# A recurrent attention kernel: its loads, its row stores and its feed-forward slots in a new order

## The chip, the cores and the metric

The kernel runs on one core of one Trainium2 chip. The metric is the device time of one execution in microseconds (us), lower is better. Engines are named as the profile names them: PE is TensorE (PEld its weight loads), DVE VectorE, ACT ScalarE, POOL GpSimd, SP SyncE, which here only issues DMA transfers.

## The reference

Two layers with residuals over x of 2048 tokens by 640. The first is attention in segments of 32 tokens with a memory of 8 rows that is handed from segment to segment, so the 64 segments are computed one after the other. The second is a feed-forward layer with a squared ReLU.

```python
# A: 32 heads of 128, 64 segments, M = 8, everything bfloat16
mem = mem0
for s in range(64):
    h = concatenate([mem, layernorm(x)[32 * s:32 * s + 32]])       # 40 x 640
    q, k, v = h @ Wq, h @ Wk, h @ Wv                                # 32 heads
    p = softmax(where(mask, q @ k.T * 128 ** -0.5, -1e9))
    o = (p @ v) @ Wo                                                # 40 x 640
    mem = o[:8]
    out_s = o[8:]
h = x + concatenate(out)
# B: 640 -> 1728 -> 640
h2 = h + relu(layernorm(h) @ w1 + b1) ** 2 @ w2 + b2
```

## The kernel before, in words

One step per segment, `step(s, ...)`, 64 steps; four steps (sp 0 to 3) make one block b of 128 tokens, 16 blocks. The memory rows and the first 24 tokens of a segment (the head rows) are 32 rows and go through the step's own chain: the Q, K and V products (`half`, `pass_units`), transposes of Q and K (`turn`), scores, exponent, sums, the product with V, and the product with Wo (`wo_units`, `wo_out`, tile `pw`, result tile `o`). Its first 8 rows are the memory of the next segment: `mem_to_hT` transposes them and puts them into hT, on which the next step's Q product waits. This chain cannot be overlapped with itself. The last 8 tokens of the four segments of a block (the tail rows) influence no memory, so they are computed for a whole block at once and ahead (`tail_units`, `tail_turn`) or behind (`wo_tail_units`, tile `psw`, result tile also tagged `o`).

Such work, and the feed-forward of an earlier block, is laid into the step's pauses. `slots` is a dictionary of lists of functions, run at named places of the step: "q" behind the Q product, "k" behind the K product, "v" and "d" behind the V product and the normalised weights, "w0" ahead of the Wo result, "w" at the end. `pre` and `mid` stand around the product with V, `post` around `mem_to_hT`. The feed-forward of one block is: load the rows of x (tile `ffh`) and of the attention's output (tile `ffa`), add them and take statistics (`ff_stats`), a reciprocal root (`ln_root`: 14 small operations on GpSimd), normalise (`ff_apply`), transpose (`ff_turn`), and eight pieces `ff_slot(b, p, tag)`, p = 0 to 7, each of two 128-wide chunks of the hidden layer: products with W1 (tile `psf`), ReLU on ScalarE, square on GpSimd (tile `f1`), products with W2 of the piece before (tile `acc`). A queue `ffq` holds these; `run_ff` takes one at two places of each step ("pv3" ahead of the Q and K transposes, "pv0" behind the weights). Each piece asks for the next W1 chunks (`ff_load1`, tile `w1c`, from w1d, a copy of W1 by chunks in DRAM) and its own W2 chunks (`ff_load2`, tile `w2c`).

Attention output goes through DRAM: each step stores its head rows (4 transfers), each block its tail rows (16 transfers), all to `a_rows`, and one transfer loads the 128 rows of a block.

Weights are loaded once. Each of Wq, Wk and Wv has 640 rows, held as five chunks of 128 partitions; the first four are four transfers, the fifth is gathered from four places: ScalarE's queue copies it to a scratch tensor `w4s` in DRAM, and SyncE's queue loads it from there. Wo comes in four transfers, two by each of these queues. W1 is copied into w1d by ten transfers issued by GpSimd behind block 0. In the last step `last_loads` loads W1 and W2 whole (tile `fw`, in the place of Wq) for the pieces that are left.

The order of the instructions of PE, ACT, DVE and POOL is the order of the code (`tc.manual_schedule`); the issues of SP are ordered by the framework's scheduler. Semaphores are set by the framework.

## Time and profile before

| | |
|---|---|
| time, median of 4 runs | 1302.85 us (1301.14 to 1304.31) |
| profiled execution: its own time, span | 1304.31 us, 1302.3 us |
| mean granted TensorE clock | 0.98 |
| busy: PE, PEld | 1088.4 us (84%), 712.3 us (55%) |
| busy: DVE, ACT, POOL | 464.2 us (36%), 414.3 us (32%), 304.3 us (23%) |
| DMA | 112.55 MB, mean 86 GB/s |

The span runs from the first to the last instruction; the execution's own time holds 2 us around it. Busy times overlap, and waiting for the serial chain is in none of them, so the table alone does not say what sets the end.

### The profile page before, as it was taken

The page shows a single profiled execution, that of the slowest core. Times are in us where ns is not written, and L with a number is a line of the kernel's source. Part 1 is how long each engine was busy: PE and PEld are TensorE (multiplying, and loading weights), DVE is VectorE, ACT ScalarE, POOL GpSimd, SP SyncE. Part 2 cuts the span into 40 slices and gives each one's busy share as a digit, 9 for nine tenths or more (in the row PEclk, how much of TensorE's full clock was granted, in tenths as well). Part 3 has the DMA queues.
Part 4 walks back from the last instruction along what each step waited for, and adds up shares of the span by engine and source line. Part 5 has one row for each costly group of instructions (what it writes and reads, how often), then busy time and mean ns, then how long its engine had stood idle before and what let it go on. Part 6 is the DMA issues. An engine that isn't in the chain of part 4 may idle for free. (4 is left out here: it accounts for less than half of the span.)

```text
span 1302.3 us, 68304 instructions
## 1 busy us (share of the span) xinstructions
PE 1088.4 (84%) x31488; PEld 712.3 (55%) x31488; DVE 464.2 (36%) x987; ACT 414.3 (32%) x848; POOL 304.3 (23%) x981
## 2 busy tenths in 40 slices
PE   0058868899899999999999899999998999989865
PEld 0025545656566655656565555656565566656543
DVE  0003333344333434344433434344443434343411
ACT  0022323334343333334333333333333333333312
POOL 3001232222221222222222222222222222222203
PEclk9998989999999999999999999999999999999978
DMA  8840031223222222223222222223222232222250
GB/s 307 306 164 6 5 93 34 73 76 91 64 75 78 75 75 73 77 71 91 67 72 77 76 81 67 73 75 91 76 72 67 76 91 65 67 69 86 77 180 18
DMA packets 97577, 112.55 MB, mean 86 GB/s; under 512 B 30731, under 2 KB 94122, under 8 KB 95322
## 3 DMA queue, kind: packets, MB, share of 16 engines
q1 hardware_dynamic: 94078, 100.19, 25.4%
q8 instruction: 246, 4.03, 1.3%
q10 hardware_dynamic: 2140, 5.77, 1.2%
q0 software_dynamic: 1072, 2.23, 0.7%
q14 instruction: 41, 0.34, 0.1%
HBM read 102.88 MB, written 10.60 MB: 87 GB/s over the span
## 5 line engine op out<-in xcount | busy, mean ns | idle before, releaser
L208 PEld LDWEIGHTS <-hT 128*32 128x32 bf16 x7680 | 204.2, 96 | 181.2 <-DVE hT L287 8.3
L227 PE MATMUL pw<-wo,oT 128*32 128x160 bf16 x8192 | 172.6, 242 | 48.8 <-issue 45.2
L227 PEld LDWEIGHTS <-oT 128*32 128x32 bf16 x8192 | 153.6, 101 | 71.9 <-issue 53.0
L208 PE MATMUL ps<-wv,hT 128*32 128x512 bf16 x2560 | 163.5, 383 | 0.0
L381 POOL TENSOR_TENSOR f<-ffr 128x128 bf16<-128x128 bf16 x224 | 84.3, 396 | 327.9 <-ACT ffr L379 276.1
L208 PE MATMUL ps<-wq,hT 128*32 128x512 bf16 x2560 | 150.1, 379 | 6.1 <-DVE hT L287 6.1
L208 PE MATMUL ps<-wk,hT 128*32 128x512 bf16 x2560 | 149.8, 379 | 0.0
L129 DVE CAST vr<-ps 128x512 bf16<-128x512 f32 x128 | 88.5, 691 | 72.0 <-PE ps L208 68.6
L379 ACT ACTIVATE ffr<-psf,b1f 128x128 bf16<-128x128 f32 x224 | 68.9, 358 | 92.3 <-PE psf L358 90.3
L129 DVE CAST qr<-ps 128x512 bf16<-128x512 f32 x64 | 44.2, 691 | 136.3 <-PE ps L208 136.3
L232 DVE CAST o<-pw 128x160 bf16<-128x160 f32 x64 | 20.7, 324 | 190.9 <-PE pw L227 183.8
L358 PE MATMUL psf<-hnT,w1c 128*128 128x128 bf16 (+1 forms) x1020 | 76.2, 220 | 9.4 <-DMA w1c<-w1d 9.3
L127 ACT COPY qT<-pt 128x1024 bf16<-128x1024 bf16 x64 | 64.8, 1012 | 57.9 <-PE pt L220 57.9
L129 DVE CAST oT<-po 128x320 bf16<-128x320 f32 x128 | 56.8, 486 | 64.7 <-PE po L486 57.0
L451 POOL TENSOR_TENSOR p<-p,mask_t 128x128 bf16<-128x128 bf16 x64 | 27.4, 428 | 223.7 <-ACT p L444 223.7
L127 ACT CAST qr<-ps 128x512 bf16<-128x512 f32 x64 | 37.5, 586 | 122.7 <-PE ps L208 122.7
L127 ACT CAST tq<-pst 128x512 bf16<-128x512 f32 x32 | 19.0, 592 | 180.1 <-PE pst L208 180.1
L358 PEld LDWEIGHTS <-w1c 128*128 128x128 bf16 (+1 forms) x1020 | 60.6, 99 | 26.6 <-issue 11.0
L370 PE MATMUL acc<-w2c,f 128*128 128x320 bf16 x404 | 72.5, 301 | 1.2 <-DMA w2c<-in_B_w_dram 1.2
L127 ACT CAST oT<-po 128x320 bf16<-128x320 f32 x128 | 48.2, 429 | 68.2 <-PE po L486 68.2
L127 ACT CAST kr<-ps 128x512 bf16<-128x512 f32 x64 | 37.5, 586 | 99.5 <-PE ps L208 99.5
L467 POOL TENSOR_TENSOR pn<-p,rk 128x128 bf16<-128x128 bf16 x64 | 42.7, 668 | 107.4 <-issue 80.8
(97 smaller groups left out, 1374.7 us busy)
## 6 DMA issues: line engine op xcount, KB each, us to landing
w1c<-w1d SPq DMA_DIRECT2D x190, 160.0 KB
w2c<-in_B_w_dram SPq DMA_DIRECT2D x188, 160.0 KB
wq<-in_A_Wq_dram SPq DMA_DIRECT2D x4, 1024.0 KB
wk<-in_A_Wk_dram SPq DMA_DIRECT2D x4, 1024.0 KB
wv<-in_A_Wv_dram SPq DMA_DIRECT2D x4, 1024.0 KB
a_rows<-o SPq DMA_DIRECT2D x256, 7.5 KB
a_rows<-o SPq DMA_DIRECT2D x256, 2.5 KB
xt<-in_A_x_dram SPq DMA_DIRECT2D x16, 160.0 KB
```

What stands on the lines that cost most here:

```text
L127: nc.scalar.copy(out=out_, in_=in_)
L129: nc.vector.tensor_copy(out=out_, in_=in_)
L208: nc.tensor.matmul(ps[32 * g:32 * g + 32, :], lhsT=lhs(c), rhs=w[:, c, g * EG + n * 512:g * EG + (n + 1) * 512], start=(c == 0), stop=(c = ...
L227: nc.tensor.matmul(ps[32 * g:32 * g + 32, 0:DG], lhsT=lhs(h), rhs=wo[:, h, g * DG:(g + 1) * DG], start=(h == 0), stop=(h == H - 1))
L232: nc.vector.tensor_copy(out=o[:], in_=ps[:, 0:DG])
L358: nc.tensor.matmul(ps[0:fs, j, :], lhsT=w1c[:, c, 0:fs], rhs=f["hnT"][:, c, :], start=(c == 0), stop=(c == DC - 1))
L370: nc.tensor.matmul(f["acc", hf][:, 0:320], lhsT=t1[0:k, :], rhs=w2c[0:k, hf * 320:(hf + 1) * 320], start=(fc == 0), stop=(fc == FC - 1))
L379: nc.scalar.activation(out=r[0:fs], in_=ps[0:fs, j, :], func=ACT.Relu, bias=b1f[0:fs, fc:fc + 1], scale=1.0)
L381: nc.gpsimd.tensor_tensor(out=t1[0:fs], in0=r[0:fs], in1=r[0:fs], op=ALU.mult)
L451: nc.gpsimd.tensor_tensor(out=p[:, :, NQ:NC], in0=p[:, :, NQ:NC], in1=mask_t[:, sp].unsqueeze(1).to_broadcast([128, HG, M + TL]), op=ALU.mult)
L467: nc.gpsimd.tensor_tensor(out=pn[:, :, NQ:NC].rearrange("p i (a q) -> p i a q", q=M), in0=p[:, :, NQ:NC].rearrange("p i (a q) -> p i a q", ...
```

## The change

- SP is added to the engines whose instructions keep the order of the code.
- The second tile of x is loaded right behind the first. The copies into w4s are cut differently (16 outer pieces in place of 4). Layer norms of blocks 0 and 1, and the feed-forward's of the last two blocks, take their root by two ScalarE operations (`ln_root_act`: Ln, then Exp of minus a half).
- `a_rows` goes. Each step stores its whole result tile to `o_d` in one transfer, each block its tail rows' tile to `ot_d` in one, and `load_rows` puts a block's 128 rows together by eight transfers; in blocks 1 to 14 in slot "d" of the second step.
- w1d is built by SP, two chunks in each of steps 0 to 6.
- The feed-forward moves: `ff_apply` from "q" to "k" of the third step, `ff_turn` from the queue to a new slot "f" between the Wo result and `mem_to_hT`, the eight pieces start with the fourth step. In the last block the feed-forward of block 14 starts with the third step, half a step earlier than before, and each step takes three pieces.
- `last_loads` is issued by GpSimd, in slot "d". The squared activations have three buffers in place of four. The tail's row loads are issued by SP and ACT in turn.
- `later`, `run_later` and the switch "now" do nothing here: nothing is put into `later`.

```diff
-    a_rows = dram.tile([S, D], BF16)
+    o_d = dram.tile([4 * NB, 128, DG], BF16)
+    ot_d = dram.tile([NB, 128, DG], BF16)
...
+    eps_t = const.tile([128, 1], F32)
+    nc.vector.memset(eps_t[:], EPS)
+
+    def ln_root_act(pool, mv):
+        rstd = pool.tile([128, 1], F32, tag="lnrs", name="lnrs")
+        nc.scalar.activation(out=rstd[:], in_=mv[:, 1:2], func=ACT.Ln, bias=eps_t[:])
+        nc.scalar.activation(out=rstd[:], in_=rstd[:], func=ACT.Exp, scale=-0.5)
+        return rstd
...
-                                                        mybir.EngineType.DVE, mybir.EngineType.Pool}))
+                                                        mybir.EngineType.DVE, mybir.EngineType.Pool,
+                                                        mybir.EngineType.SP}))
...
-            xt = s1.tile([128, D], BF16, tag="xt", name="xt")
+            xt = s2.tile([128, D], BF16, tag="ffh", name="xt") if b == 1 else s1.tile([128, D], BF16, tag="xt", name="xt")
...
+        load_x(1)
...
         for wi, src in enumerate((A_Wq, A_Wk, A_Wv)):
-            nc.scalar.dma_start(out=w4s[wi].rearrange("(g r) f -> g r f", g=G),
-                                in_=src.rearrange("(g q) h e -> g q (h e)", g=G)[:, 128:DG, :])
+            nc.scalar.dma_start(out=w4s[wi].rearrange("(g r t) f -> r g t f", g=G, t=2),
+                                in_=src.rearrange("(g q) h e -> g q (h e)", g=G)[:, 128:DG, :].rearrange(
+                                    "g (r t) f -> r g t f", t=2))
...
-        nc.vector.tensor_copy(out=b1f[:], in_=b1b[:])
...
-            roots[b] = (mv, ln_root(s1, mv))
+            roots[b] = (mv, (ln_root_act if b < 2 else ln_root)(s1, mv))
...
-                        for g in range(G):
-                            for sp in range(4):
-                                r0 = b * 128 + sp * SEG + HD
-                                nc.sync.dma_start(out=a_rows[r0:r0 + TL, g * DG:(g + 1) * DG],
-                                                  in_=ot[32 * g + sp * TL:32 * g + (sp + 1) * TL, :])
+                        nc.sync.dma_start(out=ot_d[b], in_=ot[:])
...
         def ff_rows(b):
-            a_ = s1.tile([128, D], BF16, tag="ffa", name="ffa")
             h_ = s2.tile([128, D], BF16, tag="ffh", name="ffh")
             nc.sync.dma_start(out=h_[:], in_=x2d[b * 128:(b + 1) * 128, :])
-            nc.sync.dma_start(out=a_[:], in_=a_rows[b * 128:(b + 1) * 128, :])
-            fst[b] = {"a": a_, "h": h_}
-
...
+        def load_rows(b, engs=(nc.sync,)):
+            rows = rows_of(b)
+            for sp in range(4):
+                engs[(2 * sp) % len(engs)].dma_start(
+                    out=rows[sp * SEG:sp * SEG + HD, :].rearrange("r (g q) -> r g q", g=G),
+                    in_=o_d[4 * b + sp].rearrange("(g r) q -> r g q", g=G)[M:SEG])
+                engs[(2 * sp + 1) % len(engs)].dma_start(
+                    out=rows[sp * SEG + HD:(sp + 1) * SEG, :].rearrange("r (g q) -> r g q", g=G),
+                    in_=ot_d[b].rearrange("(g s r) q -> s r g q", g=G, s=4)[sp])
...
+        def ff_stats(b, act=False):
...
-            nc.vector.tensor_tensor(out=f["h"][:], in0=f["a"][:], in1=f["h"][:], op=ALU.add)
+            nc.vector.tensor_tensor(out=f["h"][:], in0=arows.pop(b)[:], in1=f["h"][:], op=ALU.add)
...
-            f["mv"], f["r"] = mv, ln_root(s1, mv)
+            f["mv"], f["r"] = mv, (ln_root_act if act else ln_root)(s1, mv)
...
-                ff_load1((p + 1) % NP)
+                if p + 1 < NP or b + 2 < NB:
+                    ff_load1((p + 1) % NP)
...
-                    t1 = s4.tile([128, 128], BF16, tag="f1", name="f1")
+                    t1 = s3.tile([128, 128], BF16, tag="f1", name="f1")
...
-                run_ff(tag)
...
-            run(first[2])
             run(slots.get("k", ()))
             run_ff("pv3")
             turn(qr, qT[:, :, :, 0:SEG], "act", psum_v, "pv0")
             turn(kr, kT[:], "dve", psum_v, "pv1")
+            run(first[2])
...
-            run_ff("pv0")
+            run_ff("pv0", "now" in slots)
             run(slots.get("d", ()))
...
-            for g in range(G):
-                nc.sync.dma_start(out=a_rows[s * SEG:s * SEG + HD, g * DG:(g + 1) * DG],
-                                  in_=o[32 * g + M:32 * g + SEG, :])
+            nc.sync.dma_start(out=o_d[s], in_=o[:])
             run(post[0])
+            run(slots.get("f", ()))
             if s + 1 < 4 * NB:
                 mem_to_hT(o, hT4s[(s + 1) // 4], (s + 1) % 4)
             run(slots.get("w", ()))
...
-        load_x(1)
...
             for c in range(DC):
-                nc.sync.dma_start(out=w1v[:, c, :], in_=B_w1[c * 128:(c + 1) * 128, :])
+                nc.gpsimd.dma_start(out=w1v[:, c, :], in_=B_w1[c * 128:(c + 1) * 128, :])
             w2v = fw[:, DC * F:DC * F + FC * D].rearrange("p (c d) -> p c d", c=FC)
-            nc.sync.dma_start(out=w2v[:, 0:FFULL, :], in_=B_w2[0:FFULL * 128, :].rearrange("(c p) d -> p c d", p=128))
-            nc.sync.dma_start(out=w2v[0:FREM, FFULL, :], in_=B_w2[FFULL * 128:F, :])
-            nc.sync.dma_start(out=w2v[FREM:FREM + 1, FFULL, :], in_=B_b2.rearrange("(o d) -> o d", o=1))
+            nc.gpsimd.dma_start(out=w2v[:, 0:FFULL, :], in_=B_w2[0:FFULL * 128, :].rearrange("(c p) d -> p c d", p=128))
+            nc.gpsimd.dma_start(out=w2v[0:FREM, FFULL, :], in_=B_w2[FFULL * 128:F, :])
+            nc.gpsimd.dma_start(out=w2v[FREM:FREM + 1, FFULL, :], in_=B_b2.rearrange("(o d) -> o d", o=1))
             whole["w1"], whole["w2"] = w1v, w2v
...
-                        pre, mid = split(tail_units(b + 1, wk, "k", 1), 2)
+                        pre, mid = split(tail_units(b + 1, wk, "k", 1), 3)
...
-                if b > 0:
+                if s == 4 * NB - 1:
+                    sl["q"].append(lambda b=b: ff_rows(b))
+                if b == 1 and sp == 0:
+                    sl["w"].append(lambda: nc.vector.tensor_copy(out=b1f[:], in_=b1b[:]))
+                if b > 0 and nxt:
                     if sp == 1:
                         sl["q"].append(lambda b=b: ff_rows(b - 1))
                         if b == 1:
-                            sl["q"].append(lambda: (ff_load1(0)))
+                            sl["q"].append(lambda: ff_load1(0))
+                        sl["d"].append(lambda b=b: load_rows(b - 1))
                         sl["w"].append(lambda b=b: ff_stats(b - 1))
                     if sp == 2:
-                        sl["q"].append(lambda b=b: ff_apply(b - 1))
-                        ffq.append(lambda tag, b=b: ff_turn(b - 1))
+                        sl["k"].append(lambda b=b: ff_apply(b - 1))
+                        sl["f"] = [lambda b=b: ff_turn(b - 1)]
+                    if sp == 3:
                         ffq.extend(lambda tag, b=b, p=p: ff_slot(b - 1, p, tag) for p in range(NP + 1))
+                elif b > 0:
+                    if sp == 0:
+                        sl["q"].append(lambda b=b: ff_rows(b - 1))
+                        sl["w"] = [lambda b=b: load_rows(b - 1)]
+                    if sp == 1:
+                        sl["q"].append(lambda b=b: ff_stats(b - 1, True))
+                        sl["k"].append(lambda b=b: ff_apply(b - 1))
+                    sl["now"] = []
+                    post = ([], [lambda: run_ff("pv3")])
+                    if sp == 1:
+                        post[1].append(lambda b=b: (ff_turn(b - 1), ffq.extend(
+                            lambda tag, b=b, p=p: ff_slot(b - 1, p, tag) for p in range(NP + 1))))
+                for fc in range(2 * s, min(2 * s + 2, FC)):
+                    sl["w0"].append(lambda fc=fc: nc.sync.dma_start(
+                        out=w1d[fc, :, :, 0:fs_of(fc)],
+                        in_=B_w1.rearrange("(c p) f -> p c f", p=128)[:, :, fc * 128:fc * 128 + fs_of(fc)]))
                 if s == 4 * NB - 1:
-                    sl["q"].append(last_loads)
+                    sl["d"].append(last_loads)
...
-            if b == 0:
-                for c in range(DC):
-                    nc.gpsimd.dma_start(out=w1d[0:FFULL, :, c, :].rearrange("f p j -> p f j"),
-                                        in_=B_w1[c * 128:(c + 1) * 128, 0:FFULL * 128].rearrange("p (f j) -> p f j", j=128))
-                    nc.gpsimd.dma_start(out=w1d[FFULL, :, c, 0:FREM], in_=B_w1[c * 128:(c + 1) * 128, FFULL * 128:F])
...
         for f in wo_tail_units(NB - 1):
             f()
-        ff_rows(NB - 1)
-        tags = ["pv3", "pv0"]
-        for k in range(len(ffq)):
-            run_ff(tags[k % 2])
-        ff_stats(NB - 1)
+        load_rows(NB - 1, (nc.sync, nc.scalar))
+        while ffq:
+            run_ff("pv3")
+        ff_stats(NB - 1, True)
         ff_apply(NB - 1)
         ff_turn(NB - 1)
+        ff_load1(0)
         for p in range(NP + 1):
-            ff_slot(NB - 1, p, tags[p % 2])
+            ff_slot(NB - 1, p, ("pv3", "pv0")[p % 2])
```

## Rows read from the trace of the kernel before

**Rows 1.** The page's slices: span in 40 equal parts, busy tenths.
```profile
PE   0058868899899999999999899999998999989865
...
PEclk9998989999999999999999999999999999999978
```

**Rows 2.** Windows: start:end, length, busy (x count) by engine, clock, DMA share, GB/s.
```profile
0.00:80.00 80.00, 5.16 (x51) 2.50 (x55) 5.44 (x25) 1.87 (x2) 12.85 (x55) 1.00 0.79 300
20.00:44.00 24.00, 0.87 (x10) 0.67 (x10) 1.29 (x5) 0.00 (x0) 2.53 (x14) 1.00 1.02 418
```

**Rows 3.** Timeline of SP, start: start us, length us, engine, line, tiles, count.
```profile
3.30 13.79 SPq L160 DMA_DIRECT2D wq<-in_A_Wq_dram  x3
...
58.87 0.43 SPq L161 DMA_DIRECT2D wq<-w4s  x1
```

**Rows 4.** Timeline of ACT, start.
```profile
52.83 0.61 ACTq L155 DMA_DIRECT2D w4s<-in_A_Wv_dram  x1
58.54 16.21 ACTq L164 DMA_DIRECT2D wo<-in_A_Wo_dram  x2
```

**Rows 5.** Timelines of DVE and PE, start; [idle before <-releaser].
```profile
52.83 0.89 DVE L105 BATCH_NORM_STATS2 lnst<-xt 128x6 f32<-128x320 bf16 x2 [27.31 <-DMA xt<-in_A_x_dram]
...
57.84 0.64 DVE L122 TENSOR_SCALAR xn<-xt,lnmv,lnrs 128x512 bf16<-128x512 bf16 x2 [3.88 <-POOL lnrs L118]
...
58.95 1.90 PE L208 MATMUL pst<-wq,hTt 128*32 128x512 bf16 x16
...
78.25 2.75 PE L208 MATMUL pst<-wq,hTt 128*32 128x512 bf16 x24 [17.41 <-DMA wq<-w4s]
...
103.60 0.72 PE L227 MATMUL pw<-wo,oT 128*32 128x160 bf16 x16 [0.55 <-ACT oT L127]
```

**Rows 6.** Timelines of POOL and PE, step 4.
```profile
162.08 1.25 POOL L589 DMA_DIRECT2D w1d<-in_B_w_dram  x1
...
170.95 0.40 PE L437 MATMUL pss<-qT,kTt 128*32 128x16 bf16 x32 [5.46 <-POOL qT L416]
```

**Rows 7.** Timelines of SP and DVE, second step of a block in the middle.
```profile
706.94 0.43 SPq L314 DMA_DIRECT2D w2c<-in_B_b_dram  x1
...
711.77 1.53 SPq L501 DMA_DIRECT2D a_rows<-o  x4
...
712.28 0.48 DVE L328 TENSOR_TENSOR ffh<-ffa,ffh 128x640 bf16<-128x640 bf16 x1
...
714.99 0.69 DVE L129 CAST qr<-ps 128x512 bf16<-128x512 f32 x1 [1.06 <-PE ps L208]
```

**Rows 8.** Timeline of PE, third step of that block.
```profile
718.34 0.45 PE L343 MATMUL pth<-ident,hn 128*128 128x128 bf16 x5 [0.59 <-DVE hn L122]
```

**Rows 9.** Timeline of all engines, from the stall in the last step on.
```profile
1259.19 1.25 PE L358 MATMUL psf<-hnT,w1c 128*128 128x128 bf16 x10 [9.29 <-DMA w1c<-w1d]
...
1262.66 4.34 PE L227 MATMUL pw<-wo,oT 128*32 128x160 bf16 x128 [0.54 <-ACT oT L127]
...
1270.01 0.33 DVE L232 CAST o<-psw 128x160 bf16<-128x160 f32 x1 [2.62 <-PE psw L227]
1270.36 5.33 SPq L276 DMA_DIRECT2D a_rows<-o  x16
...
1277.66 0.34 SPq L321 DMA_DIRECT2D ffa<-a_rows  x1
1280.01 0.49 DVE L328 TENSOR_TENSOR ffh<-ffa,ffh 128x640 bf16<-128x640 bf16 x1 [2.98 <-issue]
...
1285.62 0.45 DVE L122 TENSOR_SCALAR hn<-ffh,ffmv,lnrs 128x640 bf16<-128x640 bf16 x1 [3.95 <-POOL lnrs L118]
...
1287.42 2.31 PE L358 MATMUL psf<-hnT,fw 128*128 128x128 bf16 x20 [0.58 <-DVE hnT L129]
```

**Rows 10.** Timeline of PE, the Wo product of a step in the middle.
```profile
670.29 2.39 PE L227 MATMUL pw<-wo,oT 128*32 128x160 bf16 x128
```

**Rows 11.** Groups by line: busy us, mean ns of one | idle before.
```profile
L464 ACT ACTIVATE rk<-rk 128x320 f32<-128x320 f32 x64 | 30.0, 469 | 2.0
```

More of the change, by code (lines that the diff above doesn't have):

```diff
@@ L131 @@
     with tc.tile_pool(name="wts", bufs=1) as wts, tc.tile_pool(name="s1", bufs=1) as s1, \
-            tc.tile_pool(name="s2", bufs=2) as s2, tc.tile_pool(name="s4", bufs=4) as s4, \
+            tc.tile_pool(name="s2", bufs=2) as s2, tc.tile_pool(name="s3", bufs=3) as s3, \
             ExitStack() as order:
         order.enter_context(tc.manual_schedule(engines={mybir.EngineType.PE, mybir.EngineType.Activation,
-                                                        mybir.EngineType.DVE, mybir.EngineType.Pool}))
+                                                        mybir.EngineType.DVE, mybir.EngineType.Pool,
+                                                        mybir.EngineType.SP}))
         wq = wts.tile([128, DC, HE], BF16, tag="wq", name="wq")
@@ L233, in wo_out, with rows_of @@
             return o
+        arows = {}
+        def rows_of(b):
+            if b not in arows:
+                arows[b] = s2.tile([128, D], BF16, tag="ffa", name="ffa")
+            return arows[b]
         def tail_row(b, which):
@@ L260, with run_stores @@
         oT = s1.tile([128, H, NQ], BF16, tag="oT")
+        stores = []
+        def run_stores(n, engs=(nc.sync,)):
+            for j in range(n):
+                stores.pop(0)(engs[j % len(engs)])
         def wo_tail_units(b):
@@ L317, in ff_rows @@
         def ff_rows(b):
-            a_ = s1.tile([128, D], BF16, tag="ffa", name="ffa")
             h_ = s2.tile([128, D], BF16, tag="ffh", name="ffh")
             nc.sync.dma_start(out=h_[:], in_=x2d[b * 128:(b + 1) * 128, :])
-            nc.sync.dma_start(out=a_[:], in_=a_rows[b * 128:(b + 1) * 128, :])
-            fst[b] = {"a": a_, "h": h_}
-        def ff_stats(b):
+            fst[b] = {"h": h_}
+        def load_rows(b, engs=(nc.sync,)):
[8 more added lines that the diff above has]
+        def ff_stats(b, act=False):
             f = fst[b]
@@ L372, in ff_slot @@
             if p < NP:
-                ff_load2(p)
+                if p > 0 or b == 0 or True:
+                    ff_load2(p)
                 for j in range(2):
@@ L392, in ff_slot, with run_ff, run_later @@
                 fst.pop(b)
-                run_ff(tag)
-        ffq = []
-        def run_ff(tag):
+        ffq, later = [], []
+        def run_ff(tag, loads=True):
             if ffq:
                 ffq.pop(0)(tag)
+            if loads:
+                run_later()
+        def run_later():
+            while later:
+                later.pop(0)()
         def step(s, first, pre, mid, post, slots):
@@ L413, in run @@
                     f()
+            run_later()
             run(first[0])
@@ L594 @@
             f()
-        ff_rows(NB - 1)
-        tags = ["pv3", "pv0"]
-        for k in range(len(ffq)):
-            run_ff(tags[k % 2])
-        ff_stats(NB - 1)
+        load_rows(NB - 1, (nc.sync, nc.scalar))
+        while ffq:
+            run_ff("pv3")
+        ff_stats(NB - 1, True)
         ff_apply(NB - 1)
         ff_turn(NB - 1)
+        ff_load1(0)
         for p in range(NP + 1):
-            ff_slot(NB - 1, p, tags[p % 2])
+            ff_slot(NB - 1, p, ("pv3", "pv0")[p % 2])
+            run_later()
 _INS = ['A_x', 'A_mem0', 'A_Wq', 'A_Wk', 'A_Wv', 'A_Wo', 'A_seg_len', 'B_x', 'B_w1', 'B_b1', 'B_w2', 'B_b2']
```

1 line of the change is left out of this document (added).

## The prediction

> **What bounds the kernel now.** I read the page's slices first: TensorE is nearly idle for two slices, sits at eight or nine tenths through the whole middle, and falls off in the last three, the last two at a lower granted clock [rows 1]. So there are three stretches: a start that waits for data, a middle that TensorE bounds, and a tail of waits. For the start I took the windows: over the first 80 us TensorE works 5.16 us while the DMA engines are 79% busy; at their best they move 418 GB/s [rows 2]. The timeline of SyncE and of ScalarE tells why the start is longer than its bytes: SyncE's Wq loads stand 13.79 us, and Wq's fifth chunk, out of the scratch tensor w4s, is asked for at 58.87 only; the last of ScalarE's three copies into w4s goes out at 52.83, and its two Wo loads stand to 74.75 [rows 3, 4]. TensorE stops in its first group and goes on at 78.25, when that chunk is in; Wo is first used 25.4 us later [rows 5]. In the middle I looked for single large waits in the table of waits and their places in the timeline: there is one, at step 4, where GpSimd issues ten transfers in a row from 162.08 and TensorE waits for its copy of qT [rows 6]. In the tail the timeline shows one stall and then a chain in which one thing runs at a time [rows 9].
>
> **The start.** The change puts SyncE's issues into the order of the code, moves the second x tile to the front, gives each w4s copy 16 outer pieces in place of 4, and takes the roots of the first two layer norms from GpSimd (DVE waited 3.88 us for one [rows 5]) to two ScalarE operations. Bytes from the code: x 0.33 MB, three w4s copies 3.15 MB, Wq, Wk, Wv and Wo 5.24 MB each. At 418 GB/s [rows 2], with 2.5 us allowed for the first transfer, Wq is whole at 2.5 + 8.72/0.418 = 23 us, Wk at 36, Wv at 48, Wo at 61.
>
> But the new root stands on ScalarE behind that engine's own DMA issues: w4s three times, then two of the four Wo loads. In this trace a load stands until earlier ones are through [rows 3, 4], and the order of issues fits a limit of eight transfers in flight, shared by both queues. If that holds, ScalarE's second Wo load is the 27th in code order and waits for the 19th, Wk's fifth chunk: ScalarE is free at 36 us. A root of this width has no row on ScalarE; it lies between nothing and two of the 320-wide Exp of 0.47 [rows 11], and I take 0.9 with the handovers, near the upper end, since even small operations have a floor. From there the first block's root takes 0.9, its normalising, transposes and copies about 2.1; the second block's chain is 6.1 us from its statistics to TensorE (52.83 to 58.95), less 3.9 of GpSimd, plus 0.9, so 3.1 [rows 5]. TensorE begins at 42 us, has its first 16 matmuls done at 44, and what stood at 78.25 stands at 44: **34 us gained**. Wo is then wanted at 44 + 25.4 = 69, and Wv before it but behind all of Wq's and Wk's products; both are in. Bounds: if ScalarE is not held, Wq's 23 us would let TensorE begin, but Wo's arrival at 61 then binds, so the point is no earlier than 36 and the gain no more than 42. If ScalarE is held until Wv is in (48), the point comes at 56: gain 22.
>
> **Step 4.** GpSimd's ten issues go; SyncE makes the same copies, two in each of steps 0 to 6, with nothing behind them on its queue that TensorE wants before step 7. The wait of 5.46 us goes [rows 6], and with it what the half clock behind it cost, a microsecond or two by that slice [rows 1]: **7 us** (5.5 to 8).
>
> **The middle.** Three moves. (a) The attention's output is stored whole (one store a step in place of four, one for the tail rows in place of 16) and put together on loading: eight loads a block in place of one. SyncE alone issues the stores and no engine waits for them in steady state, so that gains nothing. The eight loads now stand behind SyncE's last weight load of the step, which ends at 707.4; at 0.38 us each (four issues in 1.53) they are out at 710.4, and a load of whole rows took 2.35 us from issue to use [rows 7, 9], so they land near 712.5. DVE reaches for them at 712.28 and has 1.06 us of idle time ahead of its next cast [rows 7]: cost nothing, or up to 1 us a block if an issue more stands. (b) The feed-forward's normalising moves behind the K casts, and its transposes into the pause between the Wo result and the next step. The wait of 0.59 us goes [rows 8], while the copy of hnT now lies ahead of hT's, an estimated 0.25 us on the path. Net 0.3 us a block, 14 blocks: **4 us**. (c) Three buffers in place of four for the squared activations: the second multiply of a slot now waits for the first two accumulations of the slot before, which TensorE issues straight behind the slot's own first products. Nothing. Bounds for the middle: 8 us gained, 14 lost (rows 1 us late in each block).
>
> **The tail.** (a) The whole W1 and W2 were loaded on SyncE's queue, in code order ahead of the next slot's weights, and TensorE stood 9.29 us for these at 1259.19. Behind that stall its clock was halved, so Wo's 128 matmuls took 4.34 us, against 2.39 at full clock [rows 9, 10]. Now GpSimd issues them, later in the step and behind the slot's own loads. Stall and slow matmuls gone, 9.3 + 2 + about 1 of other slow work, less one slot (some 1.4 us) that now runs ahead of the last product: 10 us. GpSimd's eight issues, at most 1.25 each [rows 6], delay its copy of oT to about when the last product wants it. (b) From the last product's cast (1270.01) to the feed-forward's first matmul (1287.42) are 17.4 us: 16 store issues, a landing of 2, a load, statistics, a GpSimd root (DVE waits 3.95), transposes [rows 9]. After: a store 0.4, its landing 2, four issues on ScalarE 1.6, landing 2, DVE's addition for the block before 0.9, statistics 1.7, root 0.9, and 1.8 to the first matmul: 11.3. Gained 6. (c) Steps 60 to 63 take a third slot each: about 1 us each in 60 to 62 beyond what fills pauses; in step 61 DVE and ScalarE also wait for rows that are asked for only at the end of step 60, about 1 us. Lost 4. Together **12 us** (6 to 16).
>
> **Sum.** 34 + 7 + 4 + 12 = 57 us off the profiled execution's 1304.3, so 1247.3. That execution stands 1.5 above the median of the four runs; I say 1248 and keep the difference in the range.
>
> **Rivals.**
> R1, ScalarE is not held at the start: the limit that I read out of the issue order may not tie the two queues together. Gain 42 in place of 34: 1240. For it: only one long wait on Wq fits the number eight cleanly.
>
> R2, ScalarE is held longer, because its Wo issue itself stands as SyncE's loads do [rows 3]: gain 22, 1260.
>
> R3, the tail's stall stays: the whole W1 and W2 are 4.4 MB, 10.6 us at 418 GB/s, and weights that go out beside them wait whichever engine issued them. The slot behind the last step wants its weights about 6 us after GpSimd begins, so some 6 of the 9.3 us would stay, and 2 of half clock: 1256. Against it: in the new order that slot's weights are asked for first. The Trainium skill (DMA: Bandwidth & Descriptors, Issuing engines are not separate DMA queues) says that transfers of all issuing engines end on the same 16 DMA engines and interleave, which speaks for it.
>
> R4, slower than before: the eight row loads move pieces of 320 bytes where the load of before moved whole rows. Should they land more than 5.3 us later than I reckon, DVE casts the next Q late by 4 us past its 1.06 of slack, TensorE has no free accumulator for K, each of 14 blocks loses 4 us, and the whole gain is gone; at 7 us late 80 us are lost, 1328. Against it: stores in the same small pieces were through 2 us behind the last of 16 issues [rows 9]. The Trainium skill (DMA: Bandwidth & Descriptors, Specifications) puts the least size for full rate at 512 bytes, which speaks for it; no row of before shows such a load.
>
> R5, the issue order comes out as it was, so the start stays: 1281 with the other terms.
>
> **Numbers.** Chances: the forecast 0.56 (its own range 1241 to 1255), R1 0.14, R2 0.14, R3 0.10, R4 0.04, R5 0.02. The range of 1236 to 1264 takes in R1 to R3 and leaves out R4, R5 and the far ends of the terms. About 0.2% (2.6 us) is what a measurement of this kernel can tell from no change: faster by more 0.94, within it 0.02 (R4 near its balance), slower 0.04.
>
> **What would show it.** Start: TensorE's long run begins near 42 us and ScalarE's first Ln near 36; at 24 it is R1, past 46 R2. Step 4: no wait of TensorE on qT. Middle: no wait of DVE for a DMA ahead of the addition into ffh, or less than 1 us; several microseconds are R4. Tail: no wait for w1c, full clock under the last Wo product, and about 11 us from the last cast to the first feed-forward matmul. The prediction is most easily wrong in when ScalarE gets through its DMA issues, and next in whether eight row loads are as quick as I reckon.

## The result, and the profile after

The changed kernel takes 1243.98 us (median of 10 runs, 1235.62 to 1248.72), the kernel before 1304.76 us in the same comparison (16 runs): a ratio of 0.9535, 95% interval 0.9515 to 0.9555. The forecast was 1248 us, range 1236 to 1264.

The profiled execution after has a span of 1240.7 us, 61.6 less than before. Taking DVE's copies into hT as marks between the steps, the two traces give:

| stretch | before | after | change | forecast |
|---|---|---|---|---|
| to the end of step 0 | 108.0 | 72.7 | -35.3 | -34 |
| steps 1 to 3 | 49.3 | 48.4 | -1.0 | 0 |
| step 4 | 26.8 | 19.6 | -7.2 | -7 |
| steps 5 to 59 | 1000.4 | 990.5 | -9.9 | -4 |
| step 60 to the end | 117.7 | 109.5 | -8.2 | -12 |

The changed kernel and five of the experiments (e1 to e4 and e8) have the same code in steps 5 to 59; there the stretch took 987.5 to 990.5 us, mean 989.0. The kernel before took 1000.4, and 1001.7 in e7, whose code there is the same, so the -10 is good to about two microseconds.

The page's 40 slices of the kernel after, against [rows 1]: one empty slice of TensorE in place of two, and the DMA engines busy for 90% or more of the first two.

```profile
PE   0778898999989899998999998899998999999975
...
PEclk9989999999999999999999999999999999999996
DMA  9920222232232223213222321322232232223362
```

The start, timelines of SP, ACT and PE, against [rows 3 to 5]:

```profile
8.63 0.37 SPq L174 DMA_DIRECT2D wq<-w4s  x1
...
33.71 1.04 ACTq L177 DMA_DIRECT2D wo<-in_A_Wo_dram  x2
34.80 0.29 ACT L127 ACTIVATE lnrs<-lnmv,eps_t 128x1 f32<-128x1 f32 x1 [32.72 <-issue]
...
40.06 4.46 PE L220 MATMUL pst<-wq,hTt 128*32 128x512 bf16 x40
...
68.02 3.91 PE L239 MATMUL pw<-wo,oT 128*32 128x160 bf16 x128 [0.53 <-ACT oT L137]
```

Wq's fifth chunk is asked for at 8.6 us in place of 58.9, and the first Ln stands on ScalarE until its own Wo loads are out, as forecast (36; it came at 34.80). TensorE's run begins at 40, forecast 42.

A block in the middle, timeline of DVE, against [rows 7, 8], and under it rows of the table of waits over the middle (us in total, times, longest):

```profile
662.59 0.32 DVE L244 CAST o<-pw 128x160 bf16<-128x160 f32 x1 [3.24 <-PE pw L239]
663.33 0.20 DVE L308 CAST hT<-pm 128x40 bf16<-128x40 f32 x1 [0.42 <-PE pm L306]
664.02 0.49 DVE L357 TENSOR_TENSOR ffh<-ffa,ffh 128x640 bf16<-128x640 bf16 x1 [0.48 <-DMA ffa<-ot_d]
...
679.03 0.32 DVE L244 CAST o<-pw 128x160 bf16<-128x160 f32 x1 [2.07 <-PE pw L239]
679.42 0.49 DVE L139 COPY hnT<-pth 128x640 bf16<-128x640 bf16 x1
679.83 0.19 DVE L308 CAST hT<-pm 128x40 bf16<-128x40 f32 x1
```

```profile
PE ps L220 <- DVE qr L139: 3.0, 5, 1.4
...
DVE ffh L357 <- DMA ffa<-ot_d: 6.8, 7, 2.0
DVE ffh L357 <- DMA o_d<-o: 6.4, 4, 2.8
```

The rows do come late in 11 of 14 blocks, and 3 us of it reach TensorE, in five waits for the cast of Q. With hnT's copy ahead of it, hT's copy starts 0.80 us behind o's (679.03 to 679.83), without it 0.74.

The tail, timelines of PE, DVE, SP and ACT, against [rows 9]:

```profile
1203.50 1.57 PE L239 MATMUL psw<-wo,oTt 128*32 128x160 bf16 x80 [0.27 <-POOL oTt L532]
1208.81 1.79 PE L239 MATMUL psw<-wo,oTt 128*32 128x160 bf16 x48 [3.74 <-issue]
...
1210.65 0.33 DVE L244 CAST o<-psw 128x160 bf16<-128x160 f32 x1 [8.26 <-PE psw L239]
1211.38 5.61 SPq L346 DMA_DIRECT2D ffa<-o_d  x4
1213.27 0.72 PE L387 MATMUL psf<-hnT,w1c 128*128 128x128 bf16 x5 [2.67 <-DMA w1c<-w1d]
1216.32 0.74 PE L387 MATMUL psf<-hnT,w1c 128*64 128x128 bf16 x5 [2.33 <-DMA w1c<-w1d]
1217.43 1.57 ACTq L349 DMA_DIRECT2D ffa<-ot_d  x4
...
1226.03 2.29 PE L387 MATMUL psf<-hnT,fw 128*128 128x128 bf16 x20 [0.67 <-DVE hnT L139]
```

The stall of 9.29 us is gone from its place, but three smaller ones stand behind the last step, and from the last cast to the feed-forward are 15.4 us, not 11.3. GpSimd asks for the whole W1 and W2 from 1198.03 to 1203.04. Under the last Wo product the granted clock is 1.00 (1198 to 1202 us), as forecast; no wait for w1c and 11 us to the feed-forward were forecast too, and did not come.

### The profile page after: what moved, and what is told of

The parts are those of the page before. It is cut to its first block, busy times and chain, and to the rows that moved or that the text cites. A ratio compares the mean times of both kernels' runs of the same rounds, so it can differ in the third digit from the quotient of the medians.

```text
span 1240.7 us, 67917 instructions
## 1 busy us (share of the span) xinstructions
PE 1083.4 (87%) x31488; PEld 710.0 (57%) x31488; DVE 465.7 (38%) x988; ACT 416.2 (34%) x856; POOL 291.5 (23%) x923
## 4 chain that ended last, share of the span: by engine, by line
PE 77%; issue 8%; DVE 5%; DMA 4%; ACT 4%; SPq 1%; POOL 0%; ACTq 0%; DVEq 0%; POOLq 0%
PE ps L220 31%; PE pw L239 12%; PE pst L220 7%; PE pt L232 6%; PE psf L387 5%; PE acc L400 4%; PE psw L239 3%; DMA wk<-in_A_Wk_dram 2%; PE po L517 2%; PE po L523 2%; PE pz L494 1%; PE pss L478 1%; DVE pn L503 1%; ACT rk L501 1%; ACT rk L500 1%
## 5 line engine op out<-in xcount | busy, mean ns | idle before, releaser
L220 PEld LDWEIGHTS <-hT 128*32 128x32 bf16 x7680 | 207.1, 96 | 181.9 <-DVE hT L308 7.3
L239 PE MATMUL pw<-wo,oT 128*32 128x160 bf16 x8192 | 166.6, 237 | 50.6 <-issue 46.2
L239 PEld LDWEIGHTS <-oT 128*32 128x32 bf16 x8192 | 148.1, 99 | 74.0 <-issue 53.6
L139 DVE CAST kr<-ps 128x512 bf16<-128x512 f32 x64 | 44.2, 691 | 74.8 <-PE ps L220 74.5
```

Source lines behind the costliest of these rows:

```text
L139: nc.vector.tensor_copy(out=out_, in_=in_)
L220: nc.tensor.matmul(ps[32 * g:32 * g + 32, :], lhsT=lhs(c), rhs=w[:, c, g * EG + n * 512:g * EG + (n + 1) * 512], start=(c == 0), stop=(c = ...
L239: nc.tensor.matmul(ps[32 * g:32 * g + 32, 0:DG], lhsT=lhs(h), rhs=wo[:, h, g * DG:(g + 1) * DG], start=(h == 0), stop=(h == H - 1))
```

## The experiments

Each is the changed kernel with an edit, but e7, which is the kernel before with one.

**e1_wo_on_sp.**

```diff
-            (nc.sync if j % 2 else nc.scalar).dma_start(out=wo[...
+            nc.sync.dma_start(out=wo[...
```

> The changed kernel with all four Wo loads issued by SyncE, so that ScalarE issues only the three copies into w4s. My theory: what holds ScalarE until 33 us in the changed kernel is its own Wo issues, which stand until Wk's fifth chunk is through; without them its first Ln comes near 19 us and TensorE's long run begins at 24 to 28 us in place of 40. But Wo itself is all in at about 65 us whoever issues it, and is first used at 68.0, so the first step can end only 2 to 4 us earlier: 1239 to 1242 where the changed kernel is at 1244. Rival: the hold is what sets the start, then all 12 to 16 us come through and the time is near 1230. Second rival: ScalarE is not held by its Wo issues, its first Ln stays near 33 us and nothing changes.

1241.59 us, ratio to before 0.9520 (0.9491 to 0.9550). Timeline of PE:

```profile
25.47 4.41 PE L220 MATMUL pst<-wq,hTt 128*32 128x512 bf16 x40
...
39.94 2.75 PE L220 MATMUL pst<-wk,hTt 128*32 128x512 bf16 x24 [2.09 <-DMA wk<-w4s]
...
67.72 1.26 PE L239 MATMUL pw<-wo,oT 128*32 128x160 bf16 x32 [3.21 <-DMA wo<-in_A_Wo_dram]
...
70.06 4.30 PE L220 MATMUL ps<-wq,hT 128*32 128x512 bf16 x40 [0.31 <-DVE hT L308]
```

The first Ln comes at 20.21 and TensorE's run begins 14.6 us earlier, so the hold was ScalarE's own Wo issues. The first step ends only 2.9 us earlier (69.8): each weight is now waited for, and Wo's last quarter is in at 67.7. Steps 1 to 3 give that back: they take 51.6 us in place of 48.4. Behind the waits the granted clock is 0.62 from 68 to 76 us, against 0.79 in the changed kernel, and step 1's first Q product takes 4.30 us where 2.34 is usual. At the end of step 3 the two kernels stand level, 121.4 against 121.1 us, so the 2.4 us between the medians are not shown to come from the start.

**e2_direct.** Besides e1's edit:

```diff
-            nc.sync.dma_start(out=w[:, 4, :], in_=w4s[wi])
+            for g in range(G):
+                nc.sync.dma_start(out=w[32 * g:32 * g + 32, 4, :], in_=w2d[g * DG + 128:(g + 1) * DG, :])
```

The three copies go.

> The kernel of the run before (all Wo loads by SyncE) and besides no scratch tensor w4s: the fifth chunks of Wq, Wk and Wv are loaded straight from their four places, twelve transfers of 32 partitions issued by SyncE, in place of three copies and three loads. My theory: with ScalarE free the start is bound by its bytes, and the copies' 3.15 MB (read 1.57, written 1.57) are 7.5 us at 418 GB/s: Wo is all in at 57 to 58 us in place of 65, and the first step ends 8 to 10 us earlier than in the changed kernel: 1234 to 1236. Rival: loads of 32 partitions use few of the DMA engines and fill the eight places in flight, so the DMA share falls below 0.9 while they run and the bytes saved are lost again: within 2 us of the run before, 1239 to 1243.

1245.41 us, 0.9556 (0.9532 to 0.9580): slower than even the rival had it, and not for its reason, since the DMA share does not fall. In the windows (columns as [rows 2]) the DMA engines are full while such loads run (16 to 24 us), and move seven tenths of what they move with whole tiles (24 to 32 us):

```profile
16.00:24.00 8.00, 2.08 (x20) 0.83 (x23) 0.00 (x0) 0.59 (x1) 0.00 (x0) 1.00 1.02 287
24.00:32.00 8.00, 7.85 (x115) 3.39 (x105) 0.93 (x2) 2.34 (x4) 0.40 (x1) 1.00 1.03 406
```

**e3_copy4.** The three copies as before, in 4 outer pieces:

```diff
-            nc.scalar.dma_start(out=w4s[wi].rearrange("(g r t) f -> r g t f", g=G, t=2), ...
+            nc.scalar.dma_start(out=w4s[wi].rearrange("(g r) f -> g r f", g=G), ...
```

> The changed kernel with the three w4s copies cut into 4 outer pieces as in the kernel before; all else stays. My theory: the finer cut is a small part of the start, since the copies run beside the weight loads and the bytes are the same. In the kernel before one copy took about 16 us; three of them then end near 16, 32 and 48 us, Wk's and Wv's fifth chunks come at most some 10 us later, and ScalarE, which waits for Wk's, begins up to 5 us later: 1244 to 1249. Rival: the cut is what made the start shorter, since SyncE's fifth-chunk load stood for its copy; then Wq's chunk comes near 25 us or later and everything behind it in the queue by as much, 10 us or more slower: 1254 and above.

1264.81 us, 0.9704 (0.9675 to 0.9732). My theory fell: the first step ends 21 us later (93.8), ScalarE's Wo loads go out at 56.78. A window of this run, and the same window of the changed kernel:

```profile
8.00:16.00 8.00, 0.00 (x0) 0.00 (x0) 0.00 (x0) 0.00 (x0) 0.05 (x1) 1.00 0.50 180
```

```profile
8.00:16.00 8.00, 0.00 (x0) 0.00 (x0) 0.00 (x0) 0.00 (x0) 0.05 (x1) 1.00 1.01 372
```

With 16 pieces the share of the DMA engines is 0.94 or more from 4 to 64 us. What a copy in 4 pieces does by itself shows in the kernel before, where the third runs almost alone from 53.1 us on. A window there, and from 53 to 60 us the row of the DMA queues for ScalarE's queue (packets, MB, share of the 16 engines):

```profile
53.10:58.00 4.90, 0.00 (x0) 0.00 (x0) 0.99 (x4) 0.00 (x0) 2.69 (x14) 1.00 0.25 108
```

```profile
q10 hardware_dynamic: 12, 0.79, 26.0%
```

So while both queues stand for a copy, three quarters of the DMA engines' time is lost. The Trainium skill (DMA: Bandwidth & Descriptors, Why a DMA increments its semaphore by 16 and not by 1) says that a transfer is spread over the largest number up to 16 that divides the outermost size on both sides, so over 4 engines here. The trace agrees: 4 of 16 engines are a share of 0.25.

**e7_before_cut16.** The kernel before with the 16 pieces, the converse.

> The kernel before with one thing changed: the three copies into w4s are cut into 16 outer pieces in place of 4. After the run that undid the cut in the changed kernel cost 21 us at the first step, my theory is that the cut is most of the start: in the kernel before the DMA engines stand at shares of 0.54 to 0.57 while a copy runs alone (8 to 16 us and 48 to 56 us), and SyncE's loads of Wq stand 13.8 us for the first copy. With the cut, the first step's memory is ready 15 to 22 us earlier than the 108.0 of the kernel before and the time is 1282 to 1289. Rival: in the old order of issues the fifth chunks stand behind Wo and the x tiles whatever the copies take, the second copy still goes out near 45 us, and the gain is under 8 us: 1296 or more.

1286.29 us, 0.9851 (0.9832 to 0.9869), 18 us faster; the first step ends at 90.9 (-17.2). So the cut alone is worth 17 to 21 of the start's 35 us, and, by subtraction, the order of the issues, the second x tile and the root together the other 14 to 18; no run takes these three apart.

**e4_early_fw.**

```diff
-                    sl["d"].append(last_loads)
+                    sl["q"].append(last_loads)
```

> The changed kernel with the whole W1 and W2 asked for earlier in the last step, behind the Q product (slot q) in place of behind the weights (slot d), still by GpSimd. My theory: in the changed kernel these 4.4 MB take the DMA engines from 1198 to 1212 us, just when the tail rows' product, the weights of the last pieces and the row loads want them: TensorE stands 3.7 us ahead of psw, 2.7 and 2.3 us for w1c, and the row loads land late. Asked for some 10 us earlier the loads end near 1203, and these waits mostly go: 5 to 8 us faster, 1236 to 1239. Rival: the same bytes then hold up the weights of the last step's own pieces, GpSimd's eight issues delay its work on that step's scores, and what is saved behind the step is lost in it: within 2 us of the changed kernel.

1247.37 us, 0.9568 (0.9547 to 0.9589): the rival's mechanism, at a higher price than its 2 us. Timeline of PE, last step:

```profile
1201.07 0.45 PE L387 MATMUL psf<-hnT,w1c 128*128 128x128 bf16 x5 [3.37 <-DMA w1c<-w1d]
1203.33 0.71 PE L387 MATMUL psf<-hnT,w1c 128*128 128x128 bf16 x5 [1.81 <-DMA w1c<-w1d]
1205.81 0.69 PE L400 MATMUL acc<-w2c,f 128*128 128x320 bf16 x2 [1.77 <-DMA w2c<-in_B_w_dram]
1208.62 0.69 PE L400 MATMUL acc<-w2c,f 128*128 128x320 bf16 x2 [2.12 <-DMA w2c<-in_B_w_dram]
```

9.1 us of waits stand in the step now. Behind it the gain is there: last cast to feed-forward is 11.9 us (1218.28 to 1230.20).

**e8_split_fw.** W1 and W2 in two halves by SyncE, each behind the issues of a piece:

```diff
-                    sl["d"].append(last_loads)
+                    sl["v"].append(last_loads1)
+                    sl["d"].append(last_loads2)
```

> The changed kernel with the whole W1 and W2 issued by SyncE in two halves: W1 in slot v of the last step, behind the issues of the first of that step's pieces, W2 in slot d, behind those of the second. My theory: what counts in the tail is whether a piece's weights are asked for ahead of a large load that is still in flight; each half is 2.2 MB, 5.3 us at 418 GB/s, and fits between two pieces. The waits for w1c (2.7 and 2.3 us), part of the 3.7 us ahead of psw and the late row loads go: from the last cast to the first feed-forward matmul 12 us in place of 15.4, and 4 to 7 us in all: 1237 to 1240. Rival: SyncE's queue then stands at eight transfers in flight, as it did in the kernel before, the third piece's weights and the store of o go out late behind it, and the wait comes back ahead of them: 1243 or slower.

1239.82 us, 0.9489 (0.9467 to 0.9510): as the theory had it. No piece waits for w1c. Timelines of PE and DVE:

```profile
1203.76 1.38 PE L239 MATMUL pw<-wo,oT 128*32 128x160 bf16 x34 [3.41 <-issue]
...
1211.32 0.33 DVE L244 CAST o<-psw 128x160 bf16<-128x160 f32 x1 [5.80 <-PE psw L239]
1222.49 2.31 PE L387 MATMUL psf<-hnT,fw 128*128 128x128 bf16 x20 [0.59 <-DVE hnT L139]
```

11.2 us from cast to feed-forward, where 11.3 were forecast for the change. From the last step on the profiled execution is 3.0 us shorter than the changed kernel's (52.9 against 55.9).

**e6_w1d_gpsimd.** w1d by GpSimd's ten issues behind block 0 again.

> The changed kernel with the copy of W1 by chunks issued by GpSimd in ten transfers behind block 0 again, in place of SyncE's two in each of steps 0 to 6. My theory: GpSimd's ten issues in a row make TensorE wait for the copy of qT at step 4 again, 5 to 6 us, with a microsecond or two of half clock behind it: step 4 goes from 19.6 us to about 26.5 and the time to 1249 to 1252. Rival: the wait at step 4 had something to do with what else was in flight then in the kernel before, the issues are quicker now, and the step stays under 22 us: 1244 to 1246.

1251.37 us, 0.9577 (0.9556 to 0.9598), as the theory had it; step 4 is 26.2 us. The wait is back to the hundredth, as in [rows 6]:

```profile
133.59 0.39 PE L474 MATMUL pss<-qT,kTt 128*32 128x16 bf16 x32 [5.46 <-POOL qT L453]
```

**e5_ff_old_place.**

```diff
-                        sl["k"].append(lambda b=b: ff_apply(b - 1))
-                        sl["f"] = [lambda b=b: ff_turn(b - 1)]
-                    if sp == 3:
+                        sl["q"].append(lambda b=b: ff_apply(b - 1))
+                        ffq.append(lambda tag, b=b: ff_turn(b - 1))
...
+                run_ff(tag)
```

The last line stands behind the last piece, as in the kernel before.

> The changed kernel with the feed-forward's normalising and transposes at their old places in blocks 1 to 14: ff_apply in slot q of the third step, ff_turn in the queue of pieces ahead of the first piece, which starts with the third step again. My theory: the middle's gain, about 10 us over steps 5 to 59, is the move of the transposes into the pause between the Wo result and the next step, where TensorE waits for that result anyway, so with the old places the middle is 7 to 10 us longer and the time 1251 to 1254. The last block is not touched, but one piece less is left for it, so about 1.5 us come back in the tail. Rival: the move is worth the 0.3 us a block of the prediction, 4 us in all, and the rest of the 10 us is scatter between executions or comes from the stores: 1246 to 1248.

1282.89 us, 0.9834 (0.9806 to 0.9862): 39 us slower than the change; neither had that. Steps 5 to 59 take 1024.2. Timelines of DVE and PE, a third step:

```profile
539.36 0.49 DVE L357 TENSOR_TENSOR ffh<-ffa,ffh 128x640 bf16<-128x640 bf16 x1 [1.60 <-DMA o_d<-o]
...
544.89 0.48 DVE L132 TENSOR_SCALAR hn<-ffh,ffmv,lnrs 128x640 bf16<-128x640 bf16 x1 [3.33 <-POOL lnrs L119]
545.29 0.68 DVE L139 CAST kr<-ps 128x512 bf16<-128x512 f32 x1
...
545.43 0.61 PE L372 MATMUL pth<-ident,hn 128*128 128x128 bf16 x5 [1.89 <-DVE hn L132]
```

Rows 1.60 late, root and hn late behind them, K's cast queued behind hn, TensorE 1.89 us idle and slow for a while after: its next transposes take 1.06 us, where 0.61 is usual. That is not R4's chain, which went by a late cast of Q; here 1.6 us reach TensorE by the normalising. In the changed kernel hn stands behind K's cast and has time.

**e9_old_place_early_rows.** e5 with the row loads half a step earlier, and **e10_early_rows**, the changed kernel with that alone:

```diff
-                        sl["d"].append(lambda b=b: load_rows(b - 1))
+                        sl["q"].append(lambda b=b: load_rows(b - 1))
```

> The run with the feed-forward's old places (1282.9 us), and the eight row loads of blocks 1 to 14 asked for earlier in the second step: slot q, behind the Q product, in place of slot d. My theory: the old places cost 39 us and not 10, because the eight row loads land 1.6 to 2.8 us late, DVE's addition and the root behind it come late by as much, and at the old place the normalising then stands ahead of the K cast and the transposes ahead of those of Q and K, so TensorE waits about 1.9 us a block and runs the matmuls behind it at half clock. Asked for half a step earlier the rows are in before DVE wants them, the wait of pth falls back to the 0.6 us of the kernel before, and 20 to 30 us come back: 1253 to 1262. Rival: the old places are dear for another reason (the queue of pieces, one more of them in each third step), then the earlier loads bring under 5 us: 1278 to 1283.

> The changed kernel with the eight row loads of blocks 1 to 14 in slot q of the second step, in place of slot d. My theory: in the changed kernel DVE waits 13 us in all for rows, of which 3 us reach TensorE (five waits for the cast of Q); the new place of the normalising hides the rest. So the earlier loads bring 1 to 4 us: 1240 to 1243. Rival: the loads then stand ahead of the weights of the piece behind them on SyncE's queue and a wait for w1c takes their place: 1245 or more.

e9: 1264.06 us, 0.9703 (0.9670 to 0.9736), 19 back of the 39, 2 us past the end of what was expected. e10: 1241.47 us, 0.9524 (0.9497 to 0.9552), 2.5 faster than the change by medians, with intervals that overlap. Rows of the table of waits of e5 and of e9:

```profile
PE pth L372 <- DVE hn L132: 18.3, 14, 1.9
```

```profile
PE pth L372 <- DVE hn L132: 11.9, 14, 1.5
```

So late rows make about half of the old place dear. The other half stays with rows in time: steps 5 to 59 are 1005.8 us in e9 and 987.7 in e10, 18 us or 1.3 a block for the place alone. The place is dearer than it was in the kernel before, with pth waits of 11.9 us in these steps for 8.1: DVE's addition starts 0.37 us behind hT's copy, not 0.12, for no reason that the profile names, and hn and pth come as much later. The granted clock of the stretch is 0.993, against 0.998 in e10.

**e11_together.** e1's, e8's and e10's edits, and the last block's row loads by SyncE alone.

> The changed kernel with four of the edits tried here: all Wo loads by SyncE, the whole W1 and W2 in two halves by SyncE, the row loads of blocks 1 to 14 in slot q of the second step, and, new, the last block's row loads by SyncE alone, so that ScalarE does not stand at its four issues ahead of the last piece's ReLU (8.6 us in the run with the halves). My theory: the gains add up, 2.5 at the start, 4 in the tail, 1 to 4 in the middle, about 1 from ScalarE: 1232 to 1237. Rival: they do not add up, since the start is bound by Wo's bytes and the tail by the chain behind the last product: 1238 to 1241.

1232.41 us, 0.9451 (0.9424 to 0.9478), 11.6 us faster than the change: by the medians the edits add up. Part by part that is not shown: in the profiled execution, the fastest of the five, the end of step 3 comes hardly earlier than in the changed kernel (120.9 against 121.1), and steps 5 to 59 take 981.4 us, 6.3 less than in e10 with the same code there, 5.5 of it in TensorE's gaps that no wait explains. ScalarE's ReLU no longer stands 8.6 us; the addition now waits 2.08 us for rows.

**e12_late_w2.** e11 with W2 at the step's end:

```diff
-                    sl["d"].append(last_loads2)
+                    post[1].append(last_loads2)
```

> The run with four edits together (1232.4 us), and the whole W2 asked for later still: behind the issues of the last step's third piece, at the step's very end, in place of slot d. It tests the gap of 3.91 us in the middle of the last Wo product, at which TensorE waits for nothing that the profile shows; such gaps stand in the Wo products of most steps with 1.2 us in the mean, 2.7 at most, and the only ones over 3 us stand beside the load of the whole weights (3.74, 3.41 and 3.91 us in three kernels). My theory: the gap grows because TensorE's own instructions come over the same DMA engines; with W2 behind the step, the gap in the Wo product falls to 2 us or less, and the next one, in the tail rows' product psw, where 2.0 us stood, grows to over 3. So at best the product's o comes 2 us earlier and the time is within 2 us of the run before: 1230 to 1233. Rival: the gap belongs to that product and stays at 3 to 4 us wherever W2 is loaded; then the time does not move, or rises by the wait for W2: 1232 to 1236.

1235.84 us, 0.9476 (0.9453 to 0.9499). Timeline of PE:

```profile
1192.98 0.80 PE L239 MATMUL pw<-wo,oT 128*32 128x160 bf16 x34 [3.23 <-issue]
...
1208.64 1.23 PE L400 MATMUL acc<-fw,f 128*128 128x320 bf16 x4 [7.13 <-DMA fw<-in_B_w_dram]
```

The gap stays in its place, as the rival had it. But W1 was still coming in at 392 GB/s from 1189 to 1191 us, when the gap opened, so the run does not part the two; and psw, from 1195.95 to 1198.86, with W2 asked for from 1197.68 on, had no gap at all, where my theory wanted over 3 us. The times do not settle the cause; the trace does, and for the theory's reason, though its forecast failed (last section). What the run also shows is that W2 was now too late for the last piece (7.13 us).

## Why the prediction was right, and where its terms were off

**Start, -34 against -35.3.** The mechanism held: ScalarE stood at its Wo issues for Wk's chunks, and e1 took the hold away. Pieces of the critical path of the changed kernel:

```profile
10.22 23.46 DMA wk<-in_A_Wk_dram
33.71 0.41 ACTq L177
```

Three things in the working were wrong and did no harm. It was the first of ScalarE's two Wo loads that stood, for one of Wk's first four chunks; the forecast had the second stand for Wk's fifth chunk, which landed at 38.9 and held SyncE's next Wo load. That the time came out all the same (34.80 for 36) is in part luck, and whether the limit of eight is the chip's or the framework's, which sets the semaphores, no run shows. The sum reckoned with 418 GB/s all through and gave the cut no price; e3 and e7 show that without the cut a copy leaves three quarters of the DMA engines' time unused and 17 to 21 us are lost. And Wo is in at 67.7, not 61. So R1, had it come, would have brought some 3 us at the end of the first step, and nothing by the end of step 3 (e1), not 8.

**Step 4, -7 against -7.2.** Shown by e6, in both directions.

**Middle, -4 against -10.** Right mechanism, a term too small. The prediction counted the wait of 0.59 us less 0.25 for hnT's copy. Rows of TensorE's table of waits in the kernel before, from 235 to 1184 us, and the one of them that is left in the changed kernel, from 141 to 1131 us:

```profile
PE pth L343 <- DVE hn L122: 6.9, 12, 0.6
PE po L480 <- DVE pn L466: 6.7, 13, 0.5
PE pm L283 <- DVE o L232: 5.6, 13, 0.4
```

```profile
PE po L517 <- DVE pn L503: 5.1, 15, 1.1
```

It left out the third row: TensorE stood 0.43 us for the cast of o ahead of `mem_to_hT` in each third step, and the transposes (0.45 us) now fill that pause, while hnT's copy costs 0.06 (0.80 less 0.74). 14 x (0.59 + 0.45 - 0.06) = 13.7. It also left out the second row: the diff puts three units of K's tail product ahead of the product with V where two stood, and TensorE's wait for the weights pn falls from 0.51 to 0.29 us in each third step, 3.1 us in all; no run takes that edit apart. Against these stand the 3.0 us that late rows cost TensorE, and 3.6 us more in its gaps that no wait explains (54.7 us in steps 5 to 59 before, 58.3 after): 13.7 + 3.1 - 3.0 - 3.6 = 10.2. R4 did not come because the rows were at most 2.8 us late for DVE, where it wanted them 5.3 us later than reckoned; at the old place even that costs 19 us (e5 against e9).

**Tail, -12 against -8.2.** The terms fared worse than their sum:

| part | before | after | change | forecast |
|---|---|---|---|---|
| steps 60 to 62 | 55.3 | 53.6 | -1.7 | +4 (c) |
| step 63 to the cast of psw | 30.2 | 25.9 | -4.3 | -10 (a) |
| to the first feed-forward matmul | 17.4 | 15.4 | -2.0 | -6 (b) |
| to the end | 14.9 | 14.7 | -0.2 | 0 |

The failing term is the claim that the slot's weights, asked for first, would escape the whole W1 and W2: R3 came in part. The stall and the slow product did go, 9.9 us up to the cast of the Wo result, and the slot behind them did escape. But between that cast and psw's lie 5.7 us more than before, most of them the gap of 3.74 us in psw, which has the same load behind it (last section); the next piece's weights were asked for at 1202.84, with those loads in flight, and waited 2.67 and 2.33 us, and the row loads were held up too (15.4 us for the chain; 11.2 and 11.9 with the load out of its way in e8 and e4, 11.3 forecast). The Trainium skill (DMA: Bandwidth & Descriptors, Issuing engines are not separate DMA queues), which the prediction set against its own forecast, agrees with these rows: GpSimd's transfers delayed SyncE's. The 4 us that (c) charged for a third slot in each step did not come: 53.6 to 55.5 us in the runs with the same code there, 55.3 and 54.8 (e7) before.

The errors of +6 in the middle and -4 in the tail nearly cancel, and inside the tail (c) gave back 6 of the 10 us that (a) and (b) missed. That the sum is nearer than its terms is luck.

## What to carry to other kernels

Price every edit of a start by itself: the cut of the DRAM copies, listed here as a detail, was half of the start's gain, and a bandwidth read from full windows holds only if all transfers are spread. Two edits can carry each other: the late row loads are nearly harmless (3 us) only through the new place of the normalising, so a change taken apart can look worse than either end. A large load late in a kernel delays whatever is asked for behind it, from any engine, TensorE's own instructions too; cut it and lay the parts behind the small loads that are wanted next (1239.8 us against 1244.0 and 1247.4).

## What was not expected of the hardware

Loads of 32 partitions hold the DMA engines full and move 287 GB/s, against 406 with whole tiles. A copy from DRAM to DRAM in 4 outer pieces moves 108 GB/s at a share of 0.25 while other loads wait for it.

TensorE stops inside its 128-matmul products for nothing that the table of waits names, 1.3 us in the mean of 46 gaps in the changed kernel. The trace shows what for: its own instructions. Two rows of the changed kernel's page:

```profile
PE 1083.4 (87%) x31488; PEld 710.0 (57%) x31488; DVE 465.7 (38%) x988; ACT 416.2 (34%) x856; POOL 291.5 (23%) x923
...
q8 instruction: 246, 4.03, 1.4%
```

The 31488 matmuls and as many weight loads are 246 times 256 instructions, and queue q8 makes 246 transfers of 16 KB. In each of the 14 traces all gaps of TensorE over 0.4 us that no wait explains lie a multiple of 256 of its instructions apart, to within one, and those 46 end 1.2 to 1.6 us after a transfer of q8 is through. In the changed kernel a transfer starts 1.05 us (median) after TensorE has begun the 256 instructions ahead of the ones it brings, and takes 1.1 us. The ones it brings are then ready some 3.6 us after that beginning, while the 128 matmuls and weight loads of a Wo product at full clock take 2.39 us [rows 10]. So a gap stands at a place that the code fixes, and its length hangs on when the transfer comes. In the 14 traces a transfer started more than 2.7 us after that beginning only with the DMA engines at a share of 0.96 or more, beside the last weights of the start and beside the whole W1 or W2: 5.28 us ahead of the gap of 3.74 us, 3.83 in e12. One gap of 3.2 to 3.9 us was seen in each of nine kernels, always beside that load (e3 and e6, with the same load, had 2.63 and 2.47); with the load earlier (e4) the late transfer (3.41 us) fell into a wait for weights, and the longest gap was 2.31. Together such gaps, 55 in all, take 70 us of the changed kernel.
